# First group's norms in two token parts, neighbouring heads in batch 0's last group, and two up products begun early, in an attention and low-rank mixer kernel

## The chip, the cores and the metric

The kernel runs on one core of one Trainium2 chip. The core has five engines that run side by side and wait for each other through semaphores: TensorE (PE, matrix products; its weight loads are counted apart as PEld), VectorE (DVE), ScalarE (ACT), GpSimd (POOL) and SyncE (SP, which here only issues transfers). Each works through its own list in order. Sixteen DMA engines move data between device memory and the core; transfers are issued from the queues of SP, ACT and POOL. The metric is the time of one execution on the device in microseconds (us), as the median of several runs.

## The reference, cut to what matters

```python
batch, n_heads, seq, head_dim = (8, 12, 448, 64)       # d_model = 768, rank = 32, d_hidden = 3072

def rmsnorm(x, g):
    return x / np.sqrt(np.mean(x * x, axis=-1, keepdims=True) + 1e-06) * g

q_n, k_n = rmsnorm(q, g_q), rmsnorm(k, g_k)
scores = np.matmul(q_n, k_n.transpose(0, 1, 3, 2)) / np.sqrt(q.shape[-1])
scores = scores - np.max(scores, axis=-1, keepdims=True)
attn = np.exp(scores)
attn = attn / (np.sum(attn, axis=-1, keepdims=True) + 1e-09)
x = np.matmul(attn, v).transpose(0, 2, 1, 3).reshape(B, S, H * D)

xt = x.transpose(0, 2, 1)
h = xt @ U @ V                                          # mixes along the 448 tokens
u = x + h.transpose(0, 2, 1)
ch = np.maximum(u @ w_ch1, 0.0) @ w_ch2
out = u + ch
```

Inputs and output are fp32. The kernel takes the matrix products in bf16 with fp32 sums.

## The kernel before

**Groups and pairs.** The 12 heads of a batch are taken in three groups of four; group `gi` is heads `4*(gi%3)` to `+3` of batch `gi//3`. The 448 tokens of a head lie on 64 partitions, seven to each, and two heads stand side by side on the 128 partitions. In a group the upper and lower half of the partitions (`a`) hold two heads, and the free axis (`c`) two more. Each group makes two *pairs*: pair `lp` holds heads `lp` and `lp + 2` of its group. Batch 0 has pairs 0 to 5.

**A group's preparation.** `load` fetches q, k (one transfer each) and v (four transfers). Then: squares (`squares`, ACT or POOL), sums over the 64 elements (`sums`, DVE), the inverse root as Ln and Exp (`roots`, ACT), the product with it, cast to bf16 (`scale`, POOL or DVE), the cast of v into `va` and `vl` (`values`, POOL), transposes on PE against an identity (`turn`), and the copies out of PSUM: `take_q` multiplies q by the product of both gains `gg`, `take_k` puts the two heads of a pair into separate halves of a `kz` buffer whose other rows are zero. Of `qT` and `kz` there are two buffers, of the staged loads three.

**Attention.** `Sc(b, pr, r)` takes two score products of 448 columns into a PSUM tile `sc` (two buffers) and ACT writes their exponentials `E`; `r` runs from 0 to 3, the last with one product. `V(b, pr, half)` multiplies E by the values, whose column of ones gives the sums, then DVE takes the reciprocal and scales into `x`. `gg` also holds the bias of the exponentials, from a bound on the scores (`prep_gains`).

**Mixer and MLP.** For batch 0, `mix_t0(lo, hi)` computes columns `lo` to `hi` of `U^T x` into `tz`, `mix(b, dt)` computes one 128-column block of `u^T` into `uT` from `tz`, `Vm` and a transposed `x`, and `mix_rows` the rows of u that the end needs. `up(b, ht)` makes one of 24 hidden blocks from six products over `uT`, with a ReLU on ACT; `down` accumulates the second layer and its result is added and stored. `u^T` needs all 12 heads of the batch, so batch 0's attention comes first, and after that the attention of the next batch is spread among the MLP of this one.

**Order.** Every engine's list is in the order in which this code calls the functions (`manual_schedule`). The prologue is written out by hand (L639 to L664); the attention of batch 0 takes its extra steps from the table `extra` (L523), keyed by pair and `r`. From `first_done` on, a loop takes from two lists, `att` and `mlp`, by costs: an attention step is taken when its summed cost is not over `due(cm)`, a share of the MLP cost so far; entries with `lambda: None` are pauses. `weights(n)` issues the next `n` transfers of the MLP weights from POOL's queue, first four of `w1`, then eight of `w2`.

**Loads.** SP issues q of group 0, then q, k of group 1, q of 2, v of 0, k of 2, v of 1 and of 2, four copies of `moe_V`, then the loads of group 3 on; ACT issues k of group 0 and the two gains; POOL issues `moe_U`, cast to bf16 on the way, in four transfers. Transfers that SP and ACT issue take eight semaphores in turn, so each waits until the one eight before it has landed.

**On POOL before the first scale**: identity, fills of `Ub`, `Vm`, `Uz` and two `tb` buffers with zeros. PE begins with 115 products of the identity (`keep_busy`, `WARM`), which compute nothing that is used.

## Time and profile before

| what | us |
|---|---|
| median of 3 runs | 606.08 (605.55 to 606.76) |
| the profiled execution | 602.04 |
| its span, first to last instruction | 600.30 |
| PE busy in the span | 586.2 |
| DVE, ACT, POOL busy | 206.6, 312.5, 158.5 |
| DMA, mean over the span | 119 GB/s |
| start of the first exponential (L366) | 12.74 |
| start of the first up product (L466) | 41.12 |

The profile is of one execution. Times count from the start of its span. "Busy" is the time in which an engine runs an instruction; the share of 16 DMA engines can pass 1 where packets overlap. The matrix engine is busy 98% of the span, but not evenly, so the stretch before the first up product is read apart from the rest. In a list in order of time each row is start, duration, engine, line, operation, output and input, the number of instructions, and in brackets how long the engine had been idle before and what ended that. L numbers are lines of the kernel before.

### The profile page before, as it was taken

The numbers are of one execution on the slowest core, as the hardware profiler recorded it, in microseconds if no ns is written. First come the engines' busy times: TensorE is split into PE (matmuls) and PEld (weight loads), VectorE is DVE, ScalarE is ACT, GpSimd is POOL, SyncE is SP. The second block draws the span as 40 slices with busy tenths as digits, with TensorE's granted clock in tenths as the row PEclk, the third lists the DMA queues.
The fourth block names the chain that finished last, engine by engine and source line by source line (L and its number), as shares of the span: only waits on it lengthen the run. The fifth ranks groups of instructions, "written<-read, shape, count | busy, mean of one in ns | idle before, by whom it ended". The sixth has DMA issues, their size and how long they took to land.

```text
span 600.3 us, 11625 instructions
## 1 busy us (share of the span) xinstructions
PE 586.2 (98%) x4807; PEld 357.9 (60%) x4807; DVE 206.6 (34%) x474; ACT 312.5 (52%) x479; POOL 158.5 (26%) x271
## 2 busy tenths in 40 slices
PE   8889999999999999999999999999999999999996
PEld 8555656655666556655566655665566655655563
DVE  6686535511343322531235321541234310320011
ACT  6857873477453776356744477346763344004300
POOL 7997633123213303303303312302312000000000
PEclk9999999999999999999999999999999999999999
DMA  9999996784295454675256746277305310230022
GB/s 257 221 243 246 242 199 160 149 204 96 53 206 107 132 124 113 112 179 123 48 134 99 189 116 139 58 174 169 50 2 89 84 27 0 54 72 2 0 54 52
DMA packets 118360, 71.70 MB, mean 119 GB/s; under 512 B 80420, under 2 KB 115108, under 8 KB 118308
## 3 DMA queue, kind: packets, MB, share of 16 engines
q1 hardware_dynamic: 108304, 61.04, 45.0%
q0 software_dynamic: 9728, 9.47, 9.5%
q8 instruction: 37, 0.61, 0.4%
q10 hardware_dynamic: 276, 0.46, 0.2%
q14 instruction: 15, 0.12, 0.1%
HBM read 52.20 MB, written 11.01 MB: 105 GB/s over the span
## 4 chain that ended last, share of the span: by engine, by line
PE 92%; DVE 3%; ACT 2%; DMA 1%; POOL 1%; issue 0%; POOLq 0%; DVEq 0%; ACTq 0%
PE po L479 36%; PE ph L466 35%; PE sc L365 9%; PE pv L382 5%; PE pm L451 2%; PE pv L378 1%; PE busy L208 1%; ACT E L366 1%; DMA qT<-qn 1%; DVE ssq L133 1%; PE pu L399 1%; PE pt L311 1%; DVE x L386 0%; DVE kz L326 0%; POOL sq L130 0%
## 5 line engine op out<-in xcount | busy, mean ns | idle before, releaser
L479 PE MATMUL po<-w2b,hT 128*128 128x384 bf16 x1344 | 241.6, 326 | 1.0 <-DVE x L386 1.0
L466 PE MATMUL ph<-uT,w1b 128*128 128x448 bf16 x1152 | 237.1, 352 | 0.0
L366 ACT ACTIVATE E<-sc,gg 128x896 bf16<-128x896 f32 x192 | 171.9, 911 | 75.3 <-PE sc L365 75.1
L479 PEld LDWEIGHTS <-hT 128*128 128x128 bf16 x1344 | 126.9, 98 | 79.2 <-DVE x L386 1.1
L466 PEld LDWEIGHTS <-w1b 128*128 128x128 bf16 x1152 | 109.7, 98 | 96.1
L468 ACT ACTIVATE hT<-ph 128x448 bf16<-128x448 f32 x192 | 104.0, 545 | 116.7 <-PE ph L466 114.6
L162 POOL TENSOR_TENSOR qn<-qf,rs 128x384 bf16<-128x384 f32 x36 | 29.9, 830 | 279.1 <-ACT rs L140 225.4
L365 PE MATMUL sc<-qT,kz 128*128 128x448 bf16 x336 | 93.7, 352 | 5.2 <-ACT E L366 3.5
L385 DVE RECIPROCAL r<-pv 128x4 f32<-128x4 f32 x96 | 17.4, 181 | 212.2 <-PE pv L382 211.7
L382 PE MATMUL pv<-va,E 128*128 128x65 bf16 x1152 | 57.2, 194 | 0.0
L487 DVE TENSOR_TENSOR ob<-po,x 128x384 f32<-128x384 f32 x48 | 26.8, 558 | 84.6 <-PE po L479 83.4
L382 PEld LDWEIGHTS <-E 128*128 128x128 bf16 x1152 | 50.5, 98 | 7.5
L133 DVE TENSOR_REDUCE ssq<-sq 128x14 f32<-128x896 f32 x47 | 48.8, 1076 | 2.2 <-ACT sq L128 1.7
L365 PEld LDWEIGHTS <-kz 128*128 128x128 bf16 x336 | 31.8, 98 | 29.1 <-issue 4.7
L378 PE MATMUL pv<-vl,E 128*128 128x130 bf16 x192 | 42.1, 219 | 0.0
L386 DVE TENSOR_TENSOR x<-pv,r 128x256 bf16<-128x256 f32 x96 | 40.8, 425 | 3.3
L139 ACT ACTIVATE rs<-ssq,eps 128x28 f32<-128x28 f32 (+1 forms) x25 | 7.9, 318 | 52.4 <-DVE ssq L133 41.1
L456 DVE TENSOR_TENSOR x<-pm,x 128x384 bf16<-128x384 f32 x48 | 26.6, 554 | 17.9 <-PE pm L451 16.8
L162 POOL TENSOR_TENSOR kp<-kf,rs 128x384 bf16<-128x384 f32 x36 | 29.9, 829 | 0.0
L378 PEld LDWEIGHTS <-E 128*128 128x128 bf16 x192 | 18.7, 97 | 8.1 <-issue 1.2
L170 POOL CAST va<-vf 128x768 bf16<-128x768 f32 x24 | 20.7, 863 | 2.0 <-DMA vf<-in_v_dram 2.0
L128 ACT ACTIVATE sq<-qf 128x896 f32<-128x896 f32 x20 | 18.8, 942 | 2.3 <-DMA qf<-in_q_dram 2.3
(84 smaller groups left out, 265.2 us busy)
## 6 DMA issues: line engine op xcount, KB each, us to landing
qf<-in_q_dram SPq DMA_DIRECT2D x24, 448.0 KB, 4.2
kf<-in_k_dram SPq DMA_DIRECT2D x23, 448.0 KB, 5.5
out_dram<-ob SPq DMA_DIRECT2D x50, 192.0 KB, 2.7
vf<-in_v_dram SPq DMA_DIRECT2D x48, 192.0 KB, 5.4
w1b<-in_moe_w_ch_dram POOLq DMA_DIRECT2D x4, 1152.0 KB, 17.1
w2b<-in_moe_w_ch_dram POOLq DMA_DIRECT2D x8, 576.0 KB, 17.5
vf<-in_v_dram SPq DMA_DIRECT2D x48, 32.0 KB, 4.9
out_dram<-ob SPq DMA_DIRECT2D x12, 96.0 KB, 2.5
```

The costliest lines, as they stand in the source:

```text
L133: nc.vector.tensor_reduce(ssqs[gi][:, i, :], sqs.pop((gi, i)), AX, ALU.add)
L162: nc.gpsimd.tensor_tensor(main.rearrange("p (t i) d -> p i t d", i=2), src[:, c, :2 * NJ].rearrange("p (i t) d -> p i t d", i=2), rs[:, c, ...
L365: nc.tensor.matmul(sc[:, i, :S], kz[:, c:c + P], qT, start=True, stop=True)
L366: nc.scalar.activation(es[(b, pr)][:, 2 * r:2 * r + n, :], sc[:, :n, :S], AF.Exp, scale=scal, bias=bias)
L378: nc.tensor.matmul(pv[:, i].rearrange("p e d -> p (e d)"), E[:, NJ, w:w + P], vl[:, lp, :], start=True, stop=False)
L382: nc.tensor.matmul(pv[:, i, e, :], E[:, e * (NJ + 1) + j, w:w + P], va[:, (lp + 2 * e) * NJ + j, :], start=False, stop=(e == 1 and j == NJ ...
L386: nc.vector.tensor_tensor(xs[b].rearrange("p i (h d) -> p i h d", d=D)[:, 2 * half:2 * half + 2, h0:h0 + 3:2, :], pv[:, :, :, :D], r.rearr ...
L456: nc.vector.tensor_tensor(dst, ph[lo:hi], x[lo:hi], ALU.add)
L466: nc.tensor.matmul(ph, w1b[:, dt, ht * P:(ht + 1) * P], uT[:, dt, off:off + S], start=(dt == 0), stop=(dt == KD - 1))
L468: nc.scalar.activation(hT[:, ht, off:off + S], ph, AF.Relu)
L479: nc.tensor.matmul(po, hT[:, ht, col:col + P], w2b[:, ht, half * HALF:(half + 1) * HALF], start=(ht == 0), stop=(ht == KH - 1))
L487: nc.vector.tensor_tensor(ob[:, h], po, urows(b, col, half), ALU.add)
```

## The change

**Group 0's norms in parts.** q and k of group 0 are loaded, squared, summed and scaled in two parts of the tokens that a partition holds, 0 to 3 and 4 to 6 (`PARTS`), all four loads from SP's queue. The roots stay whole for q and for k. `gg` is copied before k's scale.

**The prologue's order.** The table load of ACT stands ahead of the gains' loads. 62 identity products instead of 115, and ten more after `prep_gains`. The product of the gains on POOL stands ahead of the fill of `Vm`; the zeros of the second `kz` buffer are written by POOL; the fills of `Uz` and `tb` come behind q's scale, followed by the first transfer of `w1`. The k square of group 1 stands behind `take_q` of group 0, the values of group 0 behind the square of group 2, and the sum for q of group 2 is in the prologue.

**U and V.** `moe_U` is loaded in fp32 by SP, into a part of an `x` buffer, and cast by DVE in `prep_u`; `moe_V` is loaded by one transfer with a repeated source instead of four.

**Batch 0's last group (`BESIDE`).** In group 2 a pair holds neighbouring heads, `2*lp` and `2*lp + 1`. Its q and k are loaded in two transfers each, of 64 partitions, and v's last tokens in another order. So pair 4 fills columns 512 to 639 of x and pair 5 the rest.

**Batch 0's end.** V products of pairs 3 and 4 come earlier, the mixer's steps later and in other slices: `tz` is computed in columns 0 to 511, 512 to 639 and 640 to 767. Two up products begin on the first four blocks of `uT` in a `sc` buffer (`up_part`), and are ended at the head of the MLP. The sum and roots for group 3 stand behind the last mix; the pause before its transposes is 1.3 instead of 1.0, with another of 0.3 behind them. In the table, scales of group 1 come one step later, POOL squares q of group 3 ahead of the values of group 2, and the transfers of `w1` are issued at other steps.

```diff
     def load_qk(gi, i, eng=None):
         b, h0, n = groups[gi]
+        if gi == BESIDE:
+            for a in range(2):
+                nc.sync.dma_start(staged[gi][i][a * R:(a + 1) * R].rearrange("p (c j) d -> p c (j d)", c=2),
+                                  (q, k)[i][b, h0 + 2 * a:h0 + 2 * a + 2].rearrange("c (p j) d -> p c (j d)", j=NT))
+            return
...
+    def squares_part(i, lo, hi):
+        if (0, i) not in sqs:
+            sqs[(0, i)] = normp.tile([P, 2 * NT, D], FP32, name="sq", tag="sq")
+        nc.scalar.activation(by_c(sqs[(0, i)])[:, :, lo:hi, :], by_c(staged[0][i])[:, :, lo:hi, :], AF.Square)
...
-    load_qk(0, 0)
-    load_qk(0, 1, nc.scalar)
+    PARTS = ((0, 4), (4, NT))
+    for i in range(2):
+        for lo, hi in PARTS:
+            load_qk_part(0, i, lo, hi)
+    nc.scalar.preload_act_table_set("natural_log_exp_and_others")
...
+    Uf = first[:, 2, :2 * (NJ + 2) * rank].bitcast(FP32).rearrange("p (j r) -> p j r", r=rank)
...
     for i in range(2):
-        nc.gpsimd.dma_start(Ub[i * R:(i + 1) * R, :NJ, :], Urows[:, i * NJ:(i + 1) * NJ, :])
+        nc.sync.dma_start(Uf[i * R:(i + 1) * R, :NJ, :], Urows[:, i * NJ:(i + 1) * NJ, :])
...
-    for m in range(NQ):
-        nc.sync.dma_start(Vf[m * rank:(m + 1) * rank, :], moe_V)
+    nc.sync.dma_start(Vf, moe_V.rearrange("(m r) s -> m r s", m=1).to_broadcast([NQ, rank, S]))
...
     def prep_u():
-        nc.vector.tensor_copy(Uz[:, :, :rank], Ub[:, :NW, :])
+        nc.vector.tensor_copy(Ub, Uf)
+        nc.vector.tensor_copy(Uz[:, :, :rank], Uf[:, :NW, :])
...
+    def up_part(b, ht, lo, hi):
+        off = 64 if b % 2 == 0 else 0
+        if not begun:
+            begin = ps_sc.tile([P, 2, 512], FP32, name="sc", tag="sc")
+            begun.update({(b, i): begin[:, i, :S] for i in range(2)})
+        ph = begun[(b, ht)]
+        for dt in range(lo, hi):
+            nc.tensor.matmul(ph, w1b[:, dt, ht * P:(ht + 1) * P], uT[:, dt, off:off + S],
+                             start=(dt == 0), stop=(dt == KD - 1))
+        if hi == KD:
+            nc.scalar.activation(hT[:, ht, off:off + S], ph, AF.Relu)
...
-        (0, 1): scales(1) + [(0, squares, (2, 1, pool)), (0, keep_busy, (8,))],
-        (0, 2): [(0, keep_busy, (8,))],
+        (0, 1): [(0, keep_busy, (8,))],
+        (0, 2): scales(1) + [(0, squares, (2, 1, pool)), (0, keep_busy, (8,))],
...
-        (1, 2): [(0, sums, (2, 0))] + turns(1),
-        (1, 3): [V2(0, 1), (0, sums, (2, 1)), (0, take_k, (1, 1)), (0, values, (1,)), (0, load, (4,)),
-                 (0, weights, (1,))],
-        (2, 1): scales(2) + [(0, weights, (1,)), V2(1, 0)],
-        (2, 3): [V2(1, 1)],
+        (1, 2): [(0.4, turn, (1, 0)), (0, take_q, (1, 0)), (0, take_q, (1, 1))],
+        (1, 3): [(0.4, turn, (1, 1)), (0, take_k, (1, 0)), V2(0, 1), (0, take_k, (1, 1)), (0, sums, (2, 1)),
+                 (0, values, (1,)), (0, load, (4,)), (0, weights, (1,))],
+        (2, 1): scales(2) + [V2(1, 0)],
+        (2, 3): [V2(1, 1), (0, prep_u, ())],
...
-        (3, 3): [V2(2, 1), (0, take_k, (2, 1)), (0, values, (2,)), (0, load, (5,)), (0, prep_v, (0, 1)), (0, prep_u, ()),
-                 (0, weights, (1,)), (0, squares, (3, 0, pool)), (0, squares, (3, 1, pool)), (0, weights, (1,))],
-        (4, 1): [V2(3, 0)],
-        (4, 3): [V2(3, 1), (0, sums, (3, 0))],
+        (3, 3): [V2(2, 1), (0, take_k, (2, 1)), (0, squares, (3, 0, pool)), (0, values, (2,)), (0, load, (5,)),
+                 (0, weights, (1,)), (0, prep_v, (0, 1)), (0, squares, (3, 1, pool)), (0, weights, (1,))],
+        (4, 0): [V2(3, 0)],
+        (4, 1): [V2(3, 1), (0, sums, (3, 0))],
         (5, 0): [(0.9, mix_t0, (0, 512))],
-        (5, 1): [V2(4, 0), (0.39, mix, (0, 0))],
-        (5, 2): [(0.39, mix, (0, 1)), (0.39, mix, (0, 2))],
-        (5, 3): [V2(4, 1), (0.39, mix, (0, 3)), (0, prep_v, (1, NQ)), (0, weights, (2,))],
+        (5, 1): [V2(4, 0)],
+        (5, 2): [V2(4, 1), (0.39, mix, (0, 0))],
+        (5, 3): [(0.39, mix, (0, 1)), (0.2, mix_t0, (512, 640)), (0, prep_v, (1, NQ)), (0, weights, (2,))],
...
-    att.extend([V2(5, 0), V2(5, 1), (0.45, mix_t0, (512, dm, True)), (0, sums, (3, 1)), (0, roots, (3,)),
-                (0.39, mix, (0, 4, True)), (0.39, mix, (0, 5))])
+    att.extend([V2(5, 0), V2(5, 1), (0.39, mix, (0, 2, True)), (0.39, mix, (0, 3, True)), (0.57, up_part, (0, 0, 0, 3)),
+                (0.2, mix_t0, (640, dm)), (0.39, mix, (0, 4, True)), (0.57, up_part, (0, 1, 0, 3)),
+                (0.39, mix, (0, 5)), (0.19, up_part, (0, 0, 3, 4)), (0.19, up_part, (0, 1, 3, 4)),
+                (0, sums, (3, 1)), (0, roots, (3,))])
...
+    for part in PARTS:
+        sums_part(1, *part)
     roots(0, 1, 2)
     pg = prep_gains()
-    scale(0, 1, nc.vector)
+    keep_busy(10)
     nc.vector.tensor_copy(gg, pg)
+    for part in PARTS:
+        scale_part(1, *part, nc.vector)
     squares(1, 0)
-    squares(1, 1)
-    values(0)
+    fill_mixer()
+    weights(1)
```

## The prediction

> **What bounds the kernel now.** I read the busy time by stretches first, then the waits of the matrix engine (PE), then the order of time of the first 42 us, and then the transfers there.
>
> ```profile
> 0.00:42.00 42.00, 35.12 (x446) 26.92 (x447) 31.05 (x89) 29.67 (x43) 35.64 (x50) 1.00 1.01 238
> 42.00:100.00 58.00, 55.59 (x491) 33.65 (x489) 31.15 (x71) 38.63 (x62) 33.84 (x44) 1.00 1.17 230
> 100.00:590.00 490.00, 490.00 (x3842) 294.25 (x3841) 143.31 (x313) 244.22 (x375) 89.01 (x179) 1.00 0.45 97
> ...
> PE sc L365 <- ACT E L366: 2.6, 6, 0.8
> ```
>
> Per stretch: PE, its weight loads, VectorE (DVE), ScalarE (ACT), GpSimd (POOL), granted clock, DMA share, GB/s. From 100 to 590 us PE is never idle, and the edit removes none of its work there. So the time is when the unbroken run of up products begins, plus the work left then. Before that PE mostly waits for exponentials, and DMA is full (1.01).
>
> ```profile
> 8.42 1.69 POOL L143 TENSOR_TENSOR qn<-qf,rs 128x896 bf16<-128x896 f32 x1 [1.27 <-ACT rs L140]
> 11.72 0.38 DVE L326 COPY kz<-pt 64x448 bf16<-64x448 bf16 x1 [0.59 <-PE pt L311]
> 12.74 1.91 ACT L366 ACTIVATE E<-sc,gg 128x896 bf16<-128x896 f32 x2 [0.32 <-PE sc L365]
> ...
> 21.67 0.90 POOL L247 DMA_DIRECT2D w1b<-in_moe_w_ch_dram  x1
> ...
> 34.74 0.36 PE L424 MATMUL ph<-Vm,x 128*128 128x448 bf16 x1 [0.62 <-DVE x L418]
> ...
> 40.33 0.36 PE L424 MATMUL ph<-Vm,x 128*128 128x448 bf16 x1 [0.46 <-ACT x L416]
> ```
>
> Start, duration, what, idle before. The first exponential starts at 12.74. The first w1 transfer is issued only at 21.67, after the loads of groups 0 to 2. PE waits round the mixer at 34.74 and 40.33; at 41.28, on the chain, the unbroken run begins.
>
> ```profile
> q0 software_dynamic: 200, 0.31, 83.8%
> q1 hardware_dynamic: 203, 0.15, 29.9%
> ...
> qf<-in_q_dram SPq DMA_DIRECT2D x1, 448.0 KB, 3.6
> ...
> qf<-in_q_dram SPq DMA_DIRECT2D x1, 448.0 KB, 9.0
> ```
>
> Packets by queue in 34 to 36 us, w1 (q0) beside SP's loads (q1): one for one, some 100 a us each. From 12 to 14 us, without w1, q1 alone moved 663. So a q load lands 3.6 us after its issue at 18.07, but 9.0 us after that at 21.74, with w1 beside it.
>
> **First group in parts.** Parts have rows of 1024 and 768 B instead of 1792. By the packet rates (420 in 2 us at 1760 B, 774 at 570 B) a packet costs about 24 ns + 0.029 ns a byte: 256 x (54 + 47) / 16 = 1.6 us for a tensor that took 1.2, and one queue carries both. I put the four landings at 4.1, 4.9, 5.8 and 6.6 us (before: q 5.6, k 5.9). A 384-element square (about 0.5) ends at 7.1, and ACT's Ln for q stands behind all four; rs of q at 7.7 (8.34 before), POOL's scale 7.75 to 9.5 (1.69 + a start), if the gains have landed by 5.1: its wait for them now stands ahead of the 1.85 us fill of Vm. They are issued about 2.0 and 2.7, behind the table load (1.28), and land 1.8 (the small V loads) to 4.5 us later (as before, behind k on their queue; the trace's semaphore record); now without k ahead, I take 2.4. DVE sums the last part by 7.6, then takes 0.6 for the gain bound; the copy of gg now stands ahead of k's scale and waits for PE (to 8.8), with both parts of that scale behind it: 8.85 to 10.6 (11.06 before). Transposing the last three blocks (0.35), copying k (0.4) and two score products (0.6) give the first exponential at 12.1, because the k square of group 1 now precedes it (11.16 to 12.1): 0.6 earlier. The roots of group 1 now stand behind three exponentials instead of two: 15.0, so POOL scales group 1 at 15.6 (15.40 before), to 18.95. Turning q meanwhile saves 0.7: scores of pair 2 at 20.0 (20.55). **Gain 0.55.**
>
> **The early w1.** POOL issues it after q's scale and the fills (1.2): at 10.7, packets some 2.2 us later as before (21.67 to 23.9), so at 12.9. Then v of groups 1 and 2 (768 packets each) is still queued. By rows, the last v part of group 1, issued about 12.3, lands between 12.3 + 6.3 (no w1) = 18.6 and 12.3 + 13.2 (beside w1) = 25.5; some 500 to 770 packets at 100 a us from 12.9, and a landing 2.5 us behind, make 22.5 to 23; I take 22.9. POOL's casts of v for group 1 wait for it: 0.65 more, then 0.9 for the second w1, and q of group 2 is scaled from 24.5 (23.72 before). The gain of 0.55 is gone: k ends at 27.85 (27.05), scores of pair 4 start at 29.2 (28.35).
>
> **The lengthened SP queue.** Every SP load waits for the one eight before it. Two more parts, halves of group 2's q and k, and U's four loads (from POOL's queue) now stand ahead of group 3's q; V's four are one. So q of group 3, issued at 18.07 before, must wait for v of group 2: by the same count landed at 24, issue at 24.3. It lands 3.6 (alone) to 9.0 or 11 (q and k beside w1) later: 27.9 to 35.3. The second w1's packets start at 25.7, so I take 8: 32.3. To this comes V. Its source is now four repeats of 32 rows. Loads of 32, 64 and 128 rows spread over all 16 DMA engines in this trace, a gain's single row over one (one late increment of its semaphore instead of 16). If 128 packets go to four engines, these carry 32 each instead of 8, right ahead of q: 24 x 0.076 = 1.8 us more alone, 24 x 0.20 = 4.8 beside w1 (157 + 160 packets in 2 us on 16 engines). No load here has four outer rows; between 0 and 4.8 I take 1.8, since the count follows the outer size in the shapes shown and V starts before the second w1. **q lands at 34.1.** By the Trainium skill (DMA: Bandwidth & Descriptors, Rules for kernel authors) an outer repeat of fewer than 16 confines a load to that many engines at most; the sum would then be nearer 36, and 2 us worse than mine; no run here shows it yet.
>
> **What waits.** POOL squares q of group 3 ahead of everything the mixer needs, so from 34.1 its queue runs: square 1.69, v casts of group 2 1.49, w1 issue 0.90, V's first block 1.16: 39.35, before which PE can't start the first mix. PE would want it at 36.0: scores of pair 4 at 29.2, then 6.8 of exponentials, scores and V products as before, the tz copy no longer behind a sum. From the mix to the unbroken run: two mixes 0.7, pair 5's V products 1.1 behind its last exponential (1.0), two mixes 0.7, six up products 1.1, tz 0.6, two mixes and two products 0.9: about 5.65. So 45.0.
>
> **The end of batch 0.** Eight up products of 0.19 are then done, 1.52 us: 45.0 - 1.52 - 41.28 = **+2.2 us**. Without the stall they and the shorter last tz slice (128 columns that wait for pair 5, instead of 256) are the real gain, since they fill PE's waits at 38.95 and 40.33. Group 3's roots now come behind the last mix; their scale (1.7) is covered by 3.4 us of up products; if that cover fails, 0.4 is lost. The longer pauses (1.0 to 1.3, 0.3) may take away the 0.48 and 0.35 waits at 46.1 and 50.4. Together -0.8 to +0.5; I take 0. Warm-up products (115 to 62, ten later) and U's fp32 copy (some 1 us on DVE) lie beside waits.
>
> The execution profiled before took 602.04 us, span 600.30; the runs' median is 606.08. I carry the change over: 602.5 span, **608.3 us**.
>
> **Rivals.** *The loads land in time* (faster): v of group 1 by 20.5 and q of group 3 by 29. For it: DMA was half idle from 16 to 20 us (111 to 116 GB/s), which w1 now fills. Against it: v4's 13 to 14 us beside w1. Then k of group 2 ends at 26.55, pair 4 starts at 27.85, the mix at 34.5, the run at 40.15: 40.15 - 1.52 - 41.28 = -2.65, **603.4**. If also the gains take 4.5 us (7.2), q's scale starts 2.1 later and the split does the opposite of what it says: 605.5. It decides from q's landing at 31.9: each us later costs one. *V on all 16 engines*: q at 32.3, +0.4 less what the pauses save: **606.2**, no change. For it: 32-row loads land in 1.8 to 2.1 us. *All four engines beside w1*: q at 37.1, +5.2: 611.3; the far end of the forecast's own mechanism.
>
> **Numbers.** The forecast with its far end 0.50, no change 0.22, loads in time 0.28. About 0.2% (1.2 us) is what this measurement tells from none: faster 0.28, same 0.22, slower 0.50. Likeliest's own range 607.3 to 611.3. The whole range reaches into the faster case, to 603.0, and to 611.2; some 0.2 stays out.
>
> **What would show it.** POOL's cast of v of group 1 with idle time before it for DMA, ending after 22.5; POOL idle several us ahead of the square of q at group 3, released by DMA qf; PE idle at the first mix for POOL Vm; the run of up products from about 45. First exponential near 12.1. The forecast is wrong if that square starts before 29, or if w1 lands by 20 with v on time.

## The result, and the profile after

The changed kernel takes 611.75 us (610.97 to 612.99, 4 runs) against 605.82 us for the kernel before (603.45 to 606.76, 4 runs): ratio 1.0105, 95% interval 1.0083 to 1.0126. The direction was forecast, the size was not: +5.9 us instead of +2.2. The profiled execution took 612.99 us with a span of 611.2; against the profiled execution of before (602.04, span 600.3) that is +10.9. The two differences are both right: the profiled execution of before was 3.8 us below its own median (the last section comes back to this).

The same three stretches as before (PE, PEld, DVE, ACT, POOL, granted clock, DMA share, GB/s):

```profile
0.00:42.00 42.00, 27.38 (x305) 19.64 (x306) 24.41 (x73) 27.11 (x39) 24.02 (x35) 0.93 0.97 210
42.00:100.00 58.00, 53.51 (x475) 32.70 (x475) 32.12 (x74) 39.30 (x64) 40.72 (x51) 0.96 1.14 212
100.00:590.00 490.00, 489.49 (x3891) 294.73 (x3890) 146.94 (x323) 247.74 (x380) 93.35 (x187) 1.00 0.46 101
```

Up to 42 us PE is busy for 27.4 us instead of 35.1, and the clock, 1.00 in all three stretches before, is 0.93. From 100 us on all is as before. The waits of PE (total, times, longest):

```profile
PE pv L417 <- POOL vl L204: 6.0, 1, 6.0
PE sc L403 <- ACT E L404: 4.7, 10, 1.1
PE pg L272 <- DVE ob L269: 2.9, 1, 2.9
PE sc L518 <- ACT hT L521: 1.5, 1, 1.5
```

Three of them are new: 6.0 us for v of group 2 at the first V products of pair 4, 2.9 in the start, 1.5 at the begun up products. The order of time on POOL shows where the 6.0 come from (start, duration, what, idle before):

```profile
12.30 1.02 POOL L282 DMA_DIRECT2D w1b<-in_moe_w_ch_dram  x1
...
26.00 0.89 POOL L282 DMA_DIRECT2D w1b<-in_moe_w_ch_dram  x1
...
40.18 1.68 POOL L146 TENSOR_TENSOR sq<-qf 128x896 f32<-128x896 f32 x1 [9.89 <-DMA qf<-in_q_dram]
```

POOL stands still for 9.89 us ahead of the square of q of group 3, and v of group 2, which PE wants, is cast behind it. The transfer itself, first in the order of time of SP's queue, then in the list of transfers (count, size, us from issue to landing), both of the changed kernel:

```profile
27.14 0.38 SPq L98 DMA_DIRECT2D qf<-in_q_dram  x1
```

```profile
qf<-in_q_dram SPq DMA_DIRECT2D x1, 448.0 KB, 12.9
```

It is issued at 27.14, 1.1 us behind w1's second transfer, and lands at 40.0. PE's own order of time:

```profile
43.26 0.27 PE L417 MATMUL pv<-vl,E 128*128 128x130 bf16 x1 [5.99 <-POOL vl L204]
...
51.23 1.23 PE L518 MATMUL sc<-uT,w1b 128*128 128x448 bf16 x4
54.14 0.54 PE L518 MATMUL sc<-uT,w1b 128*128 128x448 bf16 x2 [1.52 <-ACT hT L521]
```

Eight up products are done at 51.6; the forecast had that at 45.0.

### The profile page after: what moved, and what is told of

Read it like the earlier page. It is cut to its first block, busy times and chain, and to the rows that moved or that the text cites. A ratio compares the mean times of both kernels' runs of the same rounds, so it can differ in the third digit from the quotient of the medians.

```text
span 611.2 us, 11556 instructions
## 1 busy us (share of the span) xinstructions
PE 586.7 (96%) x4768; PEld 356.7 (58%) x4768; DVE 206.3 (34%) x474; ACT 314.2 (51%) x482; POOL 158.1 (26%) x272
## 4 chain that ended last, share of the span: by engine, by line
PE 89%; DMA 4%; DVE 2%; ACT 2%; POOL 1%; issue 0%; SPq 0%; POOLq 0%; DVEq 0%
PE po L532 35%; PE ph L505 34%; PE sc L403 9%; PE pv L421 5%; DMA vf<-in_v_dram 2%; PE pv L417 2%; PE pm L490 2%; DMA kf<-in_k_dram 1%; ACT E L404 1%; DMA qT<-qn 1%; DVE ssq L165 1%; PE pu L438 1%; PE pt L349 1%; POOL qn L175 0%; DVE kz L364 0%
## 5 line engine op out<-in xcount | busy, mean ns | idle before, releaser
L505 PE MATMUL ph<-uT,w1b 128*128 128x448 bf16 x1140 | 234.4, 352 | 0.0
L505 PEld LDWEIGHTS <-w1b 128*128 128x128 bf16 x1140 | 108.4, 98 | 95.9 <-issue 0.6
L194 POOL TENSOR_TENSOR qn<-qf,rs 128x384 bf16<-128x384 f32 x36 | 29.9, 831 | 277.2 <-ACT rs L172 259.1
L540 DVE TENSOR_TENSOR ob<-po,x 128x384 f32<-128x384 f32 x48 | 26.8, 558 | 91.4 <-PE po L532 91.1
L165 DVE TENSOR_REDUCE ssq<-sq 128x14 f32<-128x896 f32 x45 | 46.7, 1076 | 6.9 <-POOL sq L146 6.8
L425 DVE TENSOR_TENSOR x<-pv,r 128x256 bf16<-128x256 f32 x96 | 40.7, 424 | 3.3
L495 DVE TENSOR_TENSOR x<-pm,x 128x384 bf16<-128x384 f32 x48 | 26.6, 554 | 18.6 <-PE pm L490 16.5
L540 DVE TENSOR_TENSOR ob<-po,u_rest 128x384 f32<-128x384 f32 x8 | 4.5, 558 | 45.9 <-PE po L532 45.9
```

Source lines behind the costliest of these rows:

```text
L165: nc.vector.tensor_reduce(ssqs[gi][:, i, :], sqs.pop((gi, i)), AX, ALU.add)
L194: nc.gpsimd.tensor_tensor(main.rearrange("p (t i) d -> p i t d", i=2), src[:, c, :2 * NJ].rearrange("p (i t) d -> p i t d", i=2), rs[:, c, ...
L425: nc.vector.tensor_tensor(xs[b].rearrange("p i (h d) -> p i h d", d=D)[:, 2 * half:2 * half + 2, h0:h0 + step + 1:step, :], pv[:, :, :, :D ...
L495: nc.vector.tensor_tensor(dst, ph[lo:hi], x[lo:hi], ALU.add)
L505: nc.tensor.matmul(ph, w1b[:, dt, ht * P:(ht + 1) * P], uT[:, dt, off:off + S], start=(dt == 0), stop=(dt == KD - 1))
L540: nc.vector.tensor_tensor(ob[:, h], po, urows(b, col, half), ALU.add)
```

## The experiments

The table has for each the median and the ratio to the kernel before in the same runs, and from its profiled execution: the issue of w1's second transfer and of q of group 3 (behind the plus sign, after how many us this q landed; left out where no view tells), the start of POOL's square of that q (POOL's idle time ahead of it), the first up product in its own PSUM tile (`ph<-uT`), and the start of the chain of 24 down products near 100 us, with PE's wait ahead of it. All ratios lie within 1.3% of 1. The runs were taken in several rounds, in which the kernel before had medians from 604.27 to 605.82, so kernels of different rounds (e, f, g, h, i) are better compared by their ratios.

| kernel | median | ratio, 95% interval | w1 / q issued + landed | square | up | chain |
|---|---|---|---|---|---|---|
| before | 605.82 | 1 | 27.0 / 18.1 + 3.6 | 31.3 | 41.1 | 92.80 (0.98) |
| after | 611.75 | 1.0105, 1.0083 to 1.0126 | 26.0 / 27.1 + 12.9 | 40.2 (9.9) | 54.5 | 103.57 (0.51) |
| e1_v_rows | 609.54 | 1.0072, 1.0051 to 1.0093 | 26.1 / 28.6 + 9.6 | 38.3 (7.9) | 52.6 | 100.98 |
| e2_w1_later | 611.88 | 1.0117, 1.0077 to 1.0156 | 27.2 / 21.0 + 7.1 | 28.2 | 44.0 | 99.88 (7.37) |
| e3_both | 610.54 | 1.0082, 1.0040 to 1.0124 | 30.7 / 24.3 + 3.8 | 31.6 | 47.4 | 100.60 (4.65) |
| e4_warm | 612.20 | 1.0123, 1.0083 to 1.0163 | 25.8 / 26.9 + 12.6 | 39.7 (9.6) | 54.4 | 102.79 |
| f5_order | 611.60 | 1.0102, 1.0074 to 1.0129 | 25.8 / 26.9 + 12.7 | 39.8 (1.5) | 54.2 | 102.64 |
| f6_roots | 613.09 | 1.0129, 1.0099 to 1.0159 | 24.9 / 26.0 + 12.9 | 39.1 (9.9) | 55.2 | 103.67 |
| f7_before_w1 | 602.00 | 0.9955, 0.9933 to 0.9976 | 21.5 / 21.0 + 4.8 | 30.1 | 40.1 | 93.12 (1.29) |
| f8_end_alone | 606.24 | 1.0036, 1.0017 to 1.0056 | 31.4 / 19.1 + 3.7 | 32.4 | 48.2 | 96.58 |
| g1_orders | 607.73 | 1.0059, 1.0034 to 1.0084 | 24.1 / 25.2 + 12.8 | 38.1 (1.4) | 46.1 | 97.68 (1.34) |
| g2_early_w1_end | 606.56 | 1.0016, 0.9984 to 1.0048 | 26.8 / 22.8 + 3.5 | 32.0 | 48.7 | 97.12 |
| g3_relu | 604.13 | 1.0006, 0.9973 to 1.0039 | 27.7 / 22.9 + 3.5 | 33.0 | 48.0 | 97.53 |
| g4_before_v4 | 603.18 | 0.9970, 0.9948 to 0.9991 | 21.5 / 17.1 + 10.9 | 30.0 | 40.1 | 93.55 (2.76) |
| h1_k_on_act | 605.33 | 1.0004, 0.9983 to 1.0025 | 25.4 / 24.4 + 3.8 | 30.7 | 48.2 | 97.25 (0.54) |
| h2_short_queue | 605.02 | 0.9995, 0.9975 to 1.0014 | 25.6 / 25.6 | 29.9 | 46.1 | 95.11 (0.50) |
| h3_mended | 609.14 | 1.0053, 1.0032 to 1.0074 | 27.4 / 19.0 | 36.1 | 47.7 | 100.25 (0.19) |
| h4_best | 603.61 | 0.9983, 0.9956 to 1.0011 | 23.9 / 24.1 + 3.8 | 31.5 | 43.2 | 93.67 (0.84) |
| i1_second_after | 610.20 | 1.0094, 1.0059 to 1.0128 | 30.4 / 26.6 + 7.6 | 34.3 (3.1) | 47.9 | 100.09 (3.62) |
| i2_second_first | 606.73 | 1.0039, 1.0012 to 1.0066 | 21.7 / 22.8 + 8.4 | 31.4 (1.5) | 46.6 | 95.48 (0.29) |

One relation holds through the table and is the key to it: the span is the start of that chain plus 507.4 to 507.8 us (before 600.3 - 92.80 = 507.5, after 611.2 - 103.57 = 507.6, e1 608.4 - 100.98 = 507.4), except where PE had waited 2.8 us or more ahead of it (509.0 to 510.5; in e2_w1_later the granted clock is 0.50 from 100 to 105 us). Where PE did not wait there, the chain mostly starts 48.4 to 48.5 us after the first up product of the column before (e1, e4, f5, f6, f8, g2): there, and to within 0.7 us in the changed kernel itself, the beginning of the up products still sets the end. Where they begin early, a wait ahead of the chain takes its place.

### V, early w1, both, the warm-up

Theory A: q of group 3 is late through early w1, the longer queue and V on four engines. Rivals: only w1 (B), the start and the clock (C), the end of the batch (D).

e1_v_rows: V in four rows again.

```diff
-    nc.sync.dma_start(Vf, moe_V.rearrange("(m r) s -> m r s", m=1).to_broadcast([NQ, rank, S]))
+    for m in range(NQ):
+        nc.sync.dma_start(Vf[m * rank:(m + 1) * rank, :], moe_V)
```

> The changed kernel with V loaded by four transfers of 32 rows instead of one of four repeats; all else as changed. Theory A (the stall comes from q of group 3, and V on four DMA engines makes its last four parts late): V's semaphores rise on 16 engines, q of group 3 lands near 36 instead of 40.1, POOL's idle time before its square falls from 9.9 to about 6, the unbroken run of up products begins about 4 us earlier, time 607.8 (ratio to before 1.003). Rival B (q is late because w1's packets share the engines, wherever V goes): q still lands at 39 to 40, time within 1 us of 611.8. Rival C (the loss lies in the front, where the clock fell and the first exponential is 1.7 us late): q may land earlier but the time falls by less than 1.5 us.

Between A and B: q lands at 38.1, 1.9 earlier, though it is issued 1.4 later, and the time falls by about as much (chain 2.6 earlier, median 2.2; the two ratio intervals just overlap).

e2_w1_later: w1's first transfer out of the start; e3_both: that and e1's edit.

```diff
     fill_mixer()
-    weights(1)
...
-        (2, 1): scales(2) + [V2(1, 0)],
+        (2, 1): scales(2) + [(0, weights, (1,)), V2(1, 0)],
```

> The changed kernel with its first two w1 transfers issued where the kernel before has them (with the casts of v of group 1 and the scales of group 2) instead of in the start. Theory A (early w1 makes v of group 1 and q of group 3 late): v of group 1 lands by 18, q of group 3 by 27, no idle time of several us on POOL before the square of q of group 3, clock never at 0.50, the unbroken run begins near 41 to 43 with eight up products done, time 603.5 to 606.5 (ratio 0.996 to 1.001). Rival C (the front costs it: late first exponential, low clock from 10 to 20 us): the run begins after 45, time 608.5 or more. Rival D (the new order at the end of the batch costs it): PE waits there in the same sum as in the changed kernel, time 609 or more.

> The changed kernel with both undone: w1 issued where it was, and V by four transfers of 32 rows. Theory A says that V's confinement only matters where q waits behind it: with w1 late, q has slack, so the time is within 0.7 us of the kernel with w1 later alone. If V's four engines cost 1.8 us by themselves on the path, it is 1.5 to 2 us faster than that one. Rival C: as with w1 later alone, 608.5 or more.

Half of A came true and its time did not. POOL squares q at 28.2 without a wait, up products begin at 44.0, 10.6 us earlier, and the median is that of the changed kernel. The rest is lost ahead of the chain and to the clock there. First PE's order of time in the kernel before, where PE already waits a little, then of e2_w1_later PE's (the view ends within the chain), VectorE's, and the list of transfers:

```profile
92.80 4.07 PE L479 MATMUL po<-w2b,hT 128*128 128x384 bf16 x24 [0.98 <-DVE x L386]
```

```profile
99.88 6.29 PE L532 MATMUL po<-w2b,hT 128*128 128x384 bf16 x20 [7.37 <-DVE x L425]
```

```profile
98.82 0.45 DVE L379 TENSOR_SCALAR qT<-qT,gg 128x896 bf16<-128x896 bf16 x1 [10.60 <-DMA qT<-qn]
```

```profile
qT<-qn SPq DMA_TRANSPOSE x1, 12.6
```

VectorE stands for 10.6 us before its product with group 6's q, which is transposed by DMA (line 372 on). Behind it are the evictions of V products (L425), whose PSUM tiles PE needs. That transpose takes 12.6 us here, 6.9 before and 5.8 after the change. In every run w2's last transfer lands within about 2 us of it (98.9 here, 90.7 before): both run on the DMA engines at the same time (share 1.3 from 80 to 100 us). So there is a second gate: VectorE's product, and behind it PE, must wait for this transpose. That it is late because w2 is still under way is argued from these times, not tested by itself. With w1 late, the DMA engines are half idle from 15 to 25 us (share 0.55 and 0.61; before 0.66 and 1.11), and that time is probably what is missing at the end. In later expectations this gate is called "w2's landing"; the row of VectorE says that the transposes beside w2 release it.

e4_warm: `WARM = 115` instead of 62.

> The changed kernel with 115 warm-up products again instead of 62; all else as changed. Rival C (the clock gate): the granted clock stays 1.00 from 10 to 20 us, first exponential 0.5 to 1.5 us earlier, and the time falls by 2 to 4 us, to 608 to 610. Theory A: the clock is 1.00 there, but q of group 3 still lands at 40.1 and PE still waits for it, so the time falls by at most 0.4 us, 611.4 to 611.8.

The clock from 10 to 15 us is repaired, the time isn't: rival C falls. First line the changed kernel, second e4_warm, columns as above:

```profile
10.00:15.00 5.00, 4.13 (x36) 2.83 (x37) 3.87 (x9) 3.75 (x6) 3.44 (x7) 0.72 1.02 165
```

```profile
10.00:15.00 5.00, 4.40 (x51) 3.38 (x51) 3.88 (x8) 4.28 (x6) 2.70 (x5) 1.00 1.13 215
```

### Orders, the end, early w1 by itself

f5_order: POOL's order of before, in the changed kernel. f6_roots: the changed kernel with the last sum and the roots of group 3 earlier. f7_before_w1: early w1 in the kernel before. f8_end_alone: the change without its start and its transfers.

```diff
-        (3, 3): [..., (0, squares, (3, 0, pool)), (0, values, (2,)), (0, load, (5,)),
-                 (0, weights, (1,)), (0, prep_v, (0, 1)), (0, squares, (3, 1, pool)), ...
+        (3, 3): [..., (0, values, (2,)), (0, load, (5,)), (0, prep_v, (0, 1)),
+                 (0, weights, (1,)), (0, squares, (3, 0, pool)), (0, squares, (3, 1, pool)), ...
```

> The changed kernel with POOL's order at its (3, 3) step as before: v of group 2, V's first block and w1's third transfer ahead of the squares of q of group 3; loads as changed. Theory A (POOL's order makes PE wait for q of group 3): q still lands near 40, but PE's wait of 6.0 us at the V products is gone, POOL now waits for V (landed 36.8), the first mix comes at 39 to 41, the unbroken run at 48 to 49, time 606 to 608.5. Rival E (what ends last is the landing of w2's last part, which held PE for 7.4 us in the kernel with w1 later): the run begins as early, but PE waits 4 us or more at the down products of the second half, time 610 or more. Rival F (VectorE's sum of group 3 stands behind the same square and holds the mix): the run not before 51, time 609 to 610.5.

VectorE's order of time in f5_order, then PE's (columns as above, the idle time before each in brackets):

```profile
41.54 1.09 DVE L165 TENSOR_REDUCE ssq<-sq 128x14 f32<-128x896 f32 x1 [6.65 <-POOL sq L146]
```

```profile
43.28 0.55 PE L463 MATMUL ph<-Vm,x 128*128 128x448 bf16 x1 [4.86 <-DVE x L457]
```

POOL now waits 1.5 us instead of 9.9, and the time is the same (611.60): the hold goes from POOL to VectorE, whose sum of the same q (moved from (4, 3) to (4, 1) by the change) stands ahead of the copy that the mix needs.

```diff
-    att.extend([V2(5, 0), V2(5, 1), (0.39, mix, (0, 2, True)), ...
+    att.extend([V2(5, 0), V2(5, 1), (0, sums, (3, 1)), (0, roots, (3,)), (0.39, mix, (0, 2, True)), ...
...
-                (0.39, mix, (0, 5)), (0.19, up_part, (0, 0, 3, 4)), (0.19, up_part, (0, 1, 3, 4)),
-                (0, sums, (3, 1)), (0, roots, (3,))])
+                (0.39, mix, (0, 5)), (0.19, up_part, (0, 0, 3, 4)), (0.19, up_part, (0, 1, 3, 4))])
```

> The changed kernel with the last sum and the roots of group 3 ahead of the last four mixes, not behind the eight up products, so that the first ReLU on ScalarE no longer stands behind them. Theory A: PE's wait of 1.5 us for hT is gone, the unbroken run begins at 52.6 instead of 54.1, time 610.2 to 610.8. Rival E (w2's landing ends last): the 1.5 us come back as a wait for w2 at the down products (0.5 becomes 2), time 611.5 to 612.

A miss: the wait for hT shrinks to 0.5 and a new one of 1.7 for the copies of u^T, also behind the roots on ScalarE, takes its place.

```diff
+    weights(1)
     values(0)
...
-        (2, 1): scales(2) + [(0, weights, (1,)), V2(1, 0)],
+        (2, 1): scales(2) + [V2(1, 0)],
```

> The kernel before with only one edit: its first w1 transfer issued in the start, right behind the fills and q's scale of group 0, the others as they are. Theory A (early w1 is harmful only where the order of the queues makes PE wait for group 3; where it isn't, it fills DMA time that lay idle from 15 to 20 us): v of group 1 lands 3 to 5 us later, q of group 3 by 32, the unbroken run begins 0 to 1.5 us later than 41.3, w2's last part lands earlier and the wait of 0.98 us at 92.8 goes: time 604.5 to 606.5 against 605.4. Rival B (early w1 by itself costs): the run begins after 44 and the time is 608.5 or more.

Faster than expected, 0.45%. This version beats both kernels (of the others only g4, which holds it, does too). POOL's order of time in f7_before_w1:

```profile
9.67 0.91 POOL L247 DMA_DIRECT2D w1b<-in_moe_w_ch_dram  x1
...
30.05 1.69 POOL L130 TENSOR_TENSOR sq<-qf 128x896 f32<-128x896 f32 x1
```

POOL comes to the square at 30.05 and need not wait for q. Early w1 by itself is a gain in the median. The profiled executions don't show where: the up products begin 1.0 us earlier than before, but the chain does not (93.12 against 92.80).

```diff
-WARM = 62
+WARM = 115
...
-    PARTS = ((0, 4), (4, NT))
-    for i in range(2):
-        for lo, hi in PARTS:
-            load_qk_part(0, i, lo, hi)
+    PARTS = ((0, NT),)
+    load_qk(0, 0)
+    load_qk(0, 1, nc.scalar)
...
-    weights(1)
```

Besides, U's loads go on POOL's queue, V is loaded in rows and w1's first transfer stands behind the scales of group 2, as in the kernel before.

> The changed kernel with its start and its transfers undone: group 0 loaded whole on two queues, 115 warm-up products, w1 issued as before, V in four rows, U's loads on POOL's queue (still fp32 and cast on VectorE); what stays is group 2's neighbouring heads, the new order at the end of batch 0 and the eight up products begun. Theory A with a second gate at w2: PE's run starts 0 to 1.5 us earlier than in the kernel before, counted with the eight products, but w2's last part lands at 92 to 96 and PE waits 2 to 5 us there; time 605 to 608. Theory A without that gate: 603.5 to 605. Rival D (the new order costs by itself): the run begins 2 us or more later and the time is 608.5 or more.

In the range, for another reason than thought: the product of the gains, which the change puts early on POOL, now waits for gains issued behind k, and U's loads and the fill of Vm stand behind it. The first exponential starts at 15.53.

### Both holds, and early w1 with the end

g1_orders: f5's order, and VectorE's first sum of group 3 next to the second.

```diff
-        (4, 1): [V2(3, 1), (0, sums, (3, 0))],
+        (4, 1): [V2(3, 1)],
...
-                (0, sums, (3, 1)), (0, roots, (3,))])
+                (0, sums, (3, 0)), (0, sums, (3, 1)), (0, roots, (3,))])
```

> The changed kernel with both holds on q of group 3 taken off the path: POOL's order at (3, 3) as in the order run, and VectorE's first sum of group 3 moved from (4, 1) behind the up products, next to the second one. Theory A (the late q only costs through the queues that wait for it): q still lands near 40, PE's wait of 4.9 us for VectorE is gone, the first mix comes at 39 to 41 and the run at 48 to 50 with eight products done, time 606 to 608.5. Rival E (w2's last landing sets the end): PE waits 3 us or more at the down products of the second half, time 610 or more.

As A says. q still comes late (it takes 12.8 us, square at 38.1), but the up products begin 8.4 us earlier and the median falls by 4.0. Some 2 us of the 8.4 are not the order's: this execution had its first exponential at 11.78 instead of 14.41, and q was issued 2.0 us earlier. The rest says that POOL's and VectorE's lists together turn a late load into a stall of PE.

g2_early_w1_end: f8 with w1 early and the product of the gains back behind the fills. g3_relu: that, with both ReLUs behind the second product.

```diff
-        if hi == KD:
-            nc.scalar.activation(hT[:, ht, off:off + S], ph, AF.Relu)
+        if hi == KD and ht == 1:
+            for i in range(2):
+                nc.scalar.activation(hT[:, i, off:off + S], begun[(b, i)], AF.Relu)
```

> The kernel with the end alone, plus w1's first transfer in the start as in the change, and the product of the gains on POOL back behind the fills (where the kernel before has it). So of the change there stay: early w1, neighbouring heads in group 2, the order at the end, the begun products. Theory A (early w1 is harmless with the short queue of loads, and the end gives nothing because the 1.5 us wait for the first ReLU eats the eight products): first exponential by 13, q of group 3 by 31, from pair 4's first exponential to the run 14.0 us as in the runs so far, w2's wait below 2 us, time 601.5 to 603.5, about the same as the kernel before with early w1 alone. Rival G (early w1 and the end together stop PE for group 3 as in the changed kernel): POOL idle several us ahead of the square, time 607 or more.

> As the run with early w1 and the end, but the ReLUs of both begun products come behind the last product of the second, since both lie in one PSUM tile and the second waits for the first one's ReLU, which stands behind group 3's roots on ScalarE. Theory A: the wait of 1.5 us for hT is gone, the run begins 1.5 us earlier, time 0.8 to 1.5 us below that run (600.3 to 602.5). Rival E (w2's landing ends last): the wait at the down products grows by as much, same time within 0.4 us.

No stall for group 3 in either, but the first exponential is at 16.6 and 17.0, so both miss their times (g2's runs go from 602.5 to 608.4; the profiled execution of g3 took 607.19, more than its median). The wait of 1.5 us for hT is gone in g3; medians 2.4 apart, intervals overlapping: the trace shows the wait go, the time alone doesn't settle it.

g4_before_v4: f7 with V in one transfer of four repeats (e1's edit the other way round).

> The kernel before with early w1, as run, and V loaded by one transfer of four repeats. Theory A (V goes over four engines and delays the parts of q of group 3 that lie on them by about 4 us, but here POOL's square of it stands behind V's first block and VectorE's sum comes two steps later, so little of it is on the path): q lands on four engines 3 to 5 us behind the other twelve, POOL idle up to 4 us ahead of its square, time 0 to 1.5 us above the kernel before with early w1 (602 to 603.5). Rival: 4 us or more above it, 606 or more, if any late q makes PE wait.

As A says: 1.2 us above f7 (the ratio intervals overlap, so it may be less), and POOL doesn't wait, though q took 10.9 us. V's form costs little where nobody waits for q.

### What makes q late

h1_k_on_act: k's two parts on ScalarE's queue, then the gains, then the table load. h2_short_queue: V in rows (e1's edit), U's four loads on POOL's queue. Both start from the changed kernel.

```diff
-            load_qk_part(0, i, lo, hi)
-    nc.scalar.preload_act_table_set("natural_log_exp_and_others")
+            load_qk_part(0, i, lo, hi, (None, nc.scalar)[i])
...
+    nc.scalar.preload_act_table_set("natural_log_exp_and_others")
```

```diff
-        nc.sync.dma_start(Uf[i * R:(i + 1) * R, :NJ, :], Urows[:, i * NJ:(i + 1) * NJ, :])
-    nc.sync.dma_start(Uf[R:P, NJ, :], Urows[:, 2 * NJ, :])
-    nc.sync.dma_start(Uf[0:R, NJ + 1, :], Urows[:, 2 * NJ, :])
+        nc.gpsimd.dma_start(Uf[i * R:(i + 1) * R, :NJ, :], Urows[:, i * NJ:(i + 1) * NJ, :])
+    nc.gpsimd.dma_start(Uf[R:P, NJ, :], Urows[:, 2 * NJ, :])
+    nc.gpsimd.dma_start(Uf[0:R, NJ + 1, :], Urows[:, 2 * NJ, :])
```

> The changed kernel with the two parts of k of group 0 issued on ScalarE's queue (then the gains, then the table load), so that two queues carry the start. Theory A (the slow start on one queue, 124 GB/s in the first 5 us against 184 before, makes all later loads of SP's queue late): about 190 GB/s in the first 5 us, first exponential at 12 to 12.8, q of group 3 issued 1 to 2 us earlier than 27.1, landing 38 to 39.5, time 609.5 to 611. Rival (the start has slack, as the run with more warm-up products showed for the clock): q lands near 40, time within 0.5 us of 611.8.

> The changed kernel with V in four rows and U's four loads on POOL's queue (fp32 still), so that only two instructions more than before stand ahead of q of group 3 on SP besides the parts. Theory A (U's four loads on SP cost their issue and their places among the eight): q of group 3 issued at 24.5 to 26 (28.6 in the run with V in rows alone), landing 34.5 to 36.5, POOL idle 4 to 6 us ahead of its square, time 606.5 to 608.5, against 609.5 with V in rows alone. Rival: q's landing is bound by w1's packets, not by its issue: landing 37.5 to 38.5, time 609 to 610.

Each alone gives all of the loss back, more than expected (h1 by four us, h2 by 1.5). In h1 the same load of q, in SP's queue and in the list of transfers, and then POOL's order of time:

```profile
24.39 0.38 SPq L98 DMA_DIRECT2D qf<-in_q_dram  x1
```

```profile
qf<-in_q_dram SPq DMA_DIRECT2D x1, 448.0 KB, 3.8
```

```profile
25.43 0.89 POOL L282 DMA_DIRECT2D w1b<-in_moe_w_ch_dram  x1
...
30.66 1.67 POOL L146 TENSOR_TENSOR sq<-qf 128x896 f32<-128x896 f32 x1
```

q is issued 2.7 us earlier than in the changed kernel and lands 11.9 earlier, 3.8 us after its issue instead of 12.9: now it is 1.0 us ahead of w1's second transfer, not 1.1 behind it. V, too, is issued earlier, at 21.69, 2.7 us ahead of q instead of 0.8. The first exponential is at 14.36, no better than in the changed kernel (14.41): the late first exponential was not the loss.

h3_mended: the changed kernel with h1's, h2's, g1's and g3's edits at once. h4_best: f7 with the end of the change and g3's ReLUs.

> The changed kernel with every hold found so far taken away: k of group 0 on ScalarE's queue, V in four rows, U on POOL's queue, POOL's order and VectorE's first sum of group 3 off the mixer's path, both ReLUs of the begun products behind the second. What stays: parts for group 0, early w1, neighbouring heads, the begun products. Theory A with the second gate: first exponential at 12 to 12.8, no wait of PE for q of group 3 or hT, the run at 40 to 42.5 with eight products done, a wait of 0.5 to 3 us at the down products for w2; time 600.5 to 603.5. If the parts or the end cost by themselves: 605 or more.

A miss: the mends don't add up. The gains come late again (first exponential 16.36), and with both sums behind the up products PE waits 1.95 us for group 3's q at 52.25, around which the clock is 0.85 (50 to 55 us) and then 0.81 (55 to 60). Whether these two make the whole loss is not shown.

> The kernel before with early w1, and of the change only the end (neighbouring heads in group 2, order at the end, begun products, with both ReLUs behind the second); start, V, U's queue and the places of group 3's squares and first sum as before. Theory A: first exponential at 12.4, the run at 40.5 to 42 with eight products done, 0.5 to 1.5 us earlier than the kernel before with early w1 alone (40.1 with none done); w2's landing near 91 takes back what goes beyond that, so time 600.5 to 602.5. Rival D (the end is worth nothing): 602 to 603.

A miss, 1.1 us above its range and no better than f7 alone: the end is not shown to be worth anything in the time.

### The race

i1_second_after (first diff): in the changed kernel only w1's second transfer goes behind the scales of group 2. i2_second_first (second diff): in h1 it goes ahead of q.

```diff
-                 (0, values, (1,)), (0, load, (4,)), (0, weights, (1,))],
-        (2, 1): scales(2) + [V2(1, 0)],
+                 (0, values, (1,)), (0, load, (4,))],
+        (2, 1): scales(2) + [(0, weights, (1,)), V2(1, 0)],
```

```diff
-        (0, 2): scales(1) + [(0, squares, (2, 1, pool)), (0, keep_busy, (8,))],
+        (0, 2): scales(1) + [(0, weights, (1,)), (0, squares, (2, 1, pool)), (0, keep_busy, (8,))],
...
-                 (0, values, (1,)), (0, load, (4,)), (0, weights, (1,))],
+                 (0, values, (1,)), (0, load, (4,))],
```

> The changed kernel with only the second w1 transfer moved: issued behind the scales of group 2 on POOL (where the kernel before has its second), not between v of group 1 and those scales. Theory H (a race: in the changed kernel this transfer is issued at 26.0, 1.1 us ahead of q of group 3 at 27.1, and q then takes 12.9 us; in the run with k on ScalarE's queue q is issued at 24.4, 1.0 us ahead of it, and takes 3.8 us): w1's second transfer is issued at about 29.3, q of group 3 near 27, lands by 32, POOL's idle time before its square falls from 9.9 to at most 1.5 us, the run of up products starts at 46.5 to 48.5, time 604.5 to 607. Rival (V's four engines or the long queue hold q by themselves): q lands at 35 or later, time 608.5 or more.

> The kernel with k of group 0 on ScalarE's queue (605.3), and its second w1 transfer issued earlier on POOL: right behind the scales of group 1 at (0, 2), some 3 us ahead of q of group 3, so that q loses the race. Theory H: q of group 3 takes 8 us or more from its issue instead of 3.8, lands at 34 or later, POOL idle 3 us or more before its square, time 608 to 611.5. Rival (the gain of that run comes from its faster start, not from the race): q lands by 31, time within 1 us of 605.3.

POOL's order of time in i1_second_after, then PE's:

```profile
30.35 0.89 POOL L282 DMA_DIRECT2D w1b<-in_moe_w_ch_dram  x1
34.34 1.67 POOL L146 TENSOR_TENSOR sq<-qf 128x896 f32<-128x896 f32 x1 [3.11 <-DVE kz L364]
```

```profile
100.09 5.47 PE L532 MATMUL po<-w2b,hT 128*128 128x384 bf16 x24 [3.62 <-DVE x L425]
```

i1: q lands 7.6 us after its issue instead of 12.9 (at 34.2; the copy named as releaser had long been done), the up products begin 6.6 us earlier, as forecast for them; but q lands later than the forecast 32, w1 is later, and the second gate takes 3.6 us back, so the time misses. i2: q takes 8.4 us instead of 3.8, as forecast, but from an issue at 22.8; it lands at 31.2, POOL waits 1.5 us, and the time rises by 1.4 instead of 3 or more. So two things, of about equal weight, decide how long this load takes, and the plus column of the table separates them. With w1's second transfer moved behind q and V left as it was, 12.9 us become 7.6 (i1); moved ahead of q in h1, 3.8 become 8.4 (i2): some 5 us for the race. With V in rows and the race left lost, 12.9 become 9.6 (e1); with q ahead of w1's next transfer, or at most 0.3 us behind it, it is 3.5 to 4.8 where V is in rows (before, e3, f7, f8, g2, g3, h4), but 7.1 and 7.6 where V on four engines was issued 0.8 us ahead of q (e2, i1): some 3 us for V. In h1 V was 2.7 us ahead, and q took 3.8. The 10.9 of g4, 4.4 us ahead of w1's second transfer, fall beside the first, issued at 9.64 and under way for 14.0 us. So the race alone doesn't make the loss. How much of a late q PE sees hangs on the lists behind it.

## Why the prediction was right and wrong

**The step that failed is the lengthened queue**: "issue at 24.3", "so I take 8: 32.3", then 1.8 for V: "q lands at 34.1". Measured: issue at 27.14, 12.9 us, landing at 40.0, outside even the far end of 37.1. Of the 5.9 us between 34.1 and 40.0, 2.8 lie in the issue, 2.2 in V (4 instead of 1.8) and 0.9 in the rest of the way (8.9 to the last of the twelve engines instead of 8). For the issue, I let q wait for v of group 2 only. U's loads ahead of it wait for places among the eight as well (the first two for 3.1 us together, for v of group 1), and these four and V then each take a turn on SP. The start on one queue moved 124 GB/s in its first 5 us against 184; in h1, with two queues there (175 GB/s), the first load of U is issued at 15.83 instead of 23.38. These delays put q behind w1's second transfer.

**V on four engines** was weighed rightly and priced low. Where other loads update their semaphore 16 times, V does so once at 27.4 and four times from 36.2 to 36.8; of q's 16 parts twelve land from 34.9 to 36.1 and four from 39.1 to 40.0, so 4 us, and e1 gives 1.9 of them back. The forecast's far end, 611.3, had this mechanism at 4.8 us; that the time came out close to it is luck in part, since the later issue is not in it. The rule of the Trainium skill that I quoted (DMA: Bandwidth & Descriptors, Rules for kernel authors: an outer repeat of fewer than 16 confines the load to at most that many engines) agrees with that trace.

**What waits.** From q's landing to the first mix 5.7 us (forecast 5.25), from there to eight products done 5.9 (5.65, though the terms named for it make 5.1, or 6.1 with the exponential): right in size. PE's wait came a step earlier than named, at pair 4's V products for POOL's cast of v (vl), not at the first mix for Vm. Not seen: VectorE's sum as a second hold (f5), and the 1.5 us for hT. Both begun products lie in one PSUM tile, and the second's last products wait for the ReLU of the first, behind group 3's roots on ScalarE. That takes back the whole "real gain" of 1.52 us: from pair 4's first exponential to the first up product in its own tile, before took 29.00 to 41.12 (12.1 us), e2_w1_later 29.60 to 43.95 (14.4 us) with twelve products of 0.19 done, net 12.1. In h4_best, with the wait gone, 30.49 to 43.16 is net 10.4.

**The sum.** +2.2, and 5.9 for q, 0.7 behind it, 1.5 for hT: 10.3 of the 10.9 between the profiled executions.

**First group in parts**: "gain 0.55" was a loss of 2.3 at pair 2's scores (22.82), as k's second part landed at 8.5, not 6.6. With the same start the first exponential lies at 11.8 in g1 and 12.3 in e2, near the forecast 12.1, and at 15.5 in e3: k's second part lands at 6.4, 6.9 and 9.1 there, so the gain is there when k is in time. (In h1 k lands at 6.0, but the gains are issued behind it, POOL's product of them comes at 7.07, and the first exponential at 14.36.) The clock followed ("lie beside waits" was wrong: 0.72 from 10 to 15 us), but e4 (for the clock) and h1 (for the first exponential) show that neither is in the time.

**Early w1** was counted as the source of harm. v of group 1 was late as said (last cast from 25.4, forecast after 22.5), but alone it is a gain (f7), and undoing it gains nothing (e2). The rival of loads that land in time, at 603.4, was too low as well: h1 and h2, where they do, are at 605. "The time is when the unbroken run of up products begins" left out the second gate. That is not what made the changed kernel slow (it waits 0.5 us there), but it takes back what e2 and i1 gain; its sign, PE's wait of 0.98 us at 92.80, was in the profile of before.

**Rivals.** V on all 16 engines, forecast at 606.2, gave 609.5 (e1). Of the signs named in the forecast, the cast of v, POOL's idle time ahead of q's square and a wait of PE behind it came; the run at 45 and the first exponential at 12.1 did not.

## What to carry to other kernels

Price a load that is moved back in a queue by who will be on the DMA engines when it is issued, not by a mean: 2.7 us later in issue was 11.9 us later in landing (the changed kernel against h1), some 5 of them for w1 and 3 to 4 for V. Before a part of a change is called the culprit, run it alone in the old kernel; the part that looked harmful here was the only one shown to help. And look for the next gate: a stall removed ahead of 44 us came back at 92 to 100 us, where the profile of before had already shown a small wait.

## What the runs showed that was not expected

The kernel before lies between 601.4 and 608.3 us over its 103 runs beside the experiments, and its mean granted clock goes with it: 0.998 to 1.000 in the 33 runs below 604 us, 0.992 to 1.000, with a median of 0.997, in the others. The profiled execution was one with 1.000. So a typical execution of before loses some us that its profile doesn't show; f7 has 8 of 10 runs at or below 602.5. Where those executions lose it was not profiled; that early w1 spares them this is a guess.

Waits of PE cost twice here. Around the 5.99 us of waiting that ended at 43.26 the clock was 0.50 from 40 to 45 us, and after the 7.37 us of e2_w1_later it was 0.50 from 100 to 105 us and the end came 510.5 us behind the chain's start instead of 507.6. By the Trainium skill (TensorE: Matmul & The Clock Gate, Part 1: The HAM clock gate) an idle window of about 3.4 us brings the half clock; the trace agrees for these two, but shows 0.72 over 5 us (10 to 15 us) after a single wait of 2.9 us as well, and in h3 0.81 over 5 us after one of 1.95 us.
